# Tile 0 of a convolution and two-layer block on one core: four rows a partition loaded, four moved across partitions by TensorE

## The chip, the cores and the metric

The kernel runs on one core of one Trainium2 chip. The metric is device time in microseconds, a median of runs; it was 696.64 us before (three runs, 696.33 to 697.31). The engines are TensorE (PE; its weight loads are PEld), VectorE (DVE), ScalarE (ACT), GpSimd (POOL) and SyncE (SP), which issues nearly all transfers.

## What is computed

```python
# batch 2, 4160 positions, 192 channels, 8 heads, 7 taps, 1024 hidden
w = softmax(weight_gen, axis=-1)                      # [2, 4160, 8, 7]
out = np.einsum('bshk,bskhg->bshg', w, x_unf)         # x_unf: the 7 latest rows of x
xk = mu_k * x + (1 - mu_k) * x_prev                   # x = out; x_prev: one position earlier
k = np.maximum(xk @ w_k, 0.0)
x = sigmoid(xr @ w_r) * (k * k @ w_v)
h = np.maximum(x @ w_in, 0.0)
return h * sigmoid(conv3(h)) @ w_out                  # conv over 3 positions
```

Every position first takes a weighted sum of seven rows of x ("tokens" below), is then mixed with the position before, and goes through two feed-forward layers.

## The kernel before

The 4160 positions are cut into ten tiles (238, 238, seven of 476, 352), each for both batches. Tile 0 has SLOTS = 2 tokens a partition: partition p holds tokens 2p and 2p + 1, and, as each token needs six rows ahead of it, L + PAD = 2 + 6 = 8 rows of 192 f32. They come in one load a batch (line 575), of 128 x 8 x 192 x 4 bytes; neighbouring partitions load six rows in common. `rows_r` has two buffers, so that tile 1's first load reuses tile 0's first buffer.

`attention` (line 569) makes each token. A product of 128 x 1344 (7 x 192) multiplies seven rows with the softmax weights `sw` (line 583), for tile 0, batch 0 on VectorE and for everything else on GpSimd, into one of two `prod` buffers. For tile 0 (and three tokens of tile 1) the seven parts are added by TensorE: seven products with the identity matrix in plain f32 (line 590, two records each in the trace), copied by ScalarE to `tok` (lines 596, 597). `mixing` (line 616) transposes the tokens, mixes them with the previous position and splits each value into two parts, high and low, that TensorE takes in its faster f32 form. `moe1_half` and `moe1` are the first layer, `moe2` the second.

The weights are loaded in pieces during the first 50 us or so (`fetch`, line 404) and split in high and low parts on ScalarE, VectorE and TensorE (`narrow`, line 433, and `split`, line 454). The piece `w_k` comes first. `softmax` (line 536) runs on VectorE for tiles 0 to 2: a TENSOR_REDUCE, a subtraction, an exponential on ScalarE, a second TENSOR_REDUCE, and so on.

PSUM has eight banks. `pa_r` (line 379) hands out pa0, pa1 and pc1 in turn until plan time 26; the sums and the transposes of tile 0 take theirs from it, in the order of the list below.

The order of work comes from a planner. Each step is put down with a plan time (`at`, line 387); these times give a first order in which buffers are handed out. `Program.schedule` (line 136) then takes all operations, finds their dependencies by overlap of regions, and plans forwards and backwards for ROUNDS rounds with costs of its own (`cost`, line 97): a GpSimd product of 1344 elements costs 0.135 + 1344 / 446 us (line 132), a VectorE one 0.065 + 1344 / 960 (line 123). These are multiplied by PACE of the engine (line 149). SLACK (line 185) is added where TensorE waits for another engine's result, and 3.507 us stand for the end of a transfer (lines 223, 234). Each engine's queue is then issued in the planned order and runs in that order on the chip.

Ahead of TensorE's first operation `warm` (line 1078) puts WARM = 26 products of 128 x 256 whose result nobody reads. `identity` (line 1001) makes the 128 x 128 identity matrix on GpSimd.

Of the kernel before, what the change touches and what calls it, by code (L numbers as in the profile page):

```python
# [12 lines left out]
ALU = mybir.AluOpType  # L13
AX = mybir.AxisListType

NB, SEQ, DM, NH, KS, DFF = 2, 4160, 192, 8, 7, 1024
# [8 lines left out]
PART = [128] * NTILE  # L25
SLOTS = [2, 2] + [4] * 7 + [3]
EXTRA = [0] + [p * l - n for p, l, n in zip(PART, SLOTS, SIZES)][1:]
PAD = KS - 1
WIN = KS * DM
NF = DFF // 128  # L30
LAG = 12
WARM = 26
SLACK = {"ACT": 0.311, "DVE": 0.274, "POOL": 0.239}
PACE = {"ACT": 1.045, "DVE": 1.035, "POOL": 1.037}
ROUNDS = 13
HELD = [85.0, 140.0, 215.0, 290.0, 365.0, 440.0, 515.0]
HIGH = range(5)
LOWS = {(NTILE - 1, NB - 1, k) for k in range(6, NF)}
# [15 lines left out]
class Program:  # L54
# [4 lines left out]
        self.ops, self.spaces = [], {}  # L59
        self.real = {"PE": nc.tensor, "ACT": nc.scalar, "DVE": nc.vector, "POOL": nc.gpsimd, "SP": nc.sync}  # L60

    warm = None

    def engine(self, name):
        program = self
# [70 lines left out]
    def schedule(self):  # L136
        n = len(self.ops)
        succ, left, ready, dur, late, moved = [[] for _ in range(n)], [0] * n, [0.0] * n, [0.0] * n, [0.0] * n, [0.0] * n
        shares = [False] * n
        log = {}  # L140
        for i, (eng, method, a, k, _, hold) in enumerate(self.ops):
            ready[i] = hold
            aps = [x for x in [*a, *k.values()] if hasattr(x, "tensor") and hasattr(x, "ap")]
            out = k["out"] if "out" in k else aps[0]
# [14 lines left out]
            for x, write in [(x, False) for x in ins] + [(out, True)]:  # L159
# [3 lines left out]
                for e in seen:  # L163
                    j, w, q0, q1, g0, g1 = e
# [16 lines left out]
        load = [op[1] == "dma_start" for op in self.ops]  # L181
        turns = [op[2][2] if op[0] == "ACT" and op[1] == "activation" and op[2][2] in (ACTF.Exp, ACTF.Sigmoid) else None
                 for op in self.ops]
        hold = ready
# [23 lines left out]
        def forward(rank):  # L208
            nonlocal when
            when = hold[:]  # L210
            start, last, table = [0.0] * n, 0.0, ACTF.Exp
            wires = dict.fromkeys(self.real, 0.0)

            def step(i, eng, t):
                nonlocal last, table
                start[i] = t
                if turns[i] is not None:
                    t = t + (0.0 if turns[i] == table else 1.3)
                    table = turns[i]
                end = t + late[i]  # L220
                if load[i]:
                    wires[eng] = max(wires[eng], t + dur[i] + 0.55) + moved[i]
                    end = wires[eng] + 3.507
                last = max(last, end)
                for j in succ[i]:
                    when[j] = max(when[j], t + dur[i] if eng in ("PE", "POOL") and eng == name[j] else end + slack(i, name[j]))
                return t

            walk((pred, succ), lambda i: (rank[i], i), step)
            return start, last  # L230

        def backward(start, last):
            nonlocal when
            full = [dur[i] + 0.55 + moved[i] + 3.507 if load[i] else late[i] for i in range(n)]
            when = [full[i] - dur[i] for i in range(n)]
            rank = [0.0] * n

            def step(i, eng, t):
                rank[i] = last - t - dur[i]
                for j in pred[i]:  # L240
                    when[j] = max(when[j], t + dur[i] - dur[j] + (dur[j] if name[j] in ("PE", "POOL") and name[j] == eng else full[j] + slack(j, eng)))
                return t

            walk((succ, pred), lambda i: (-start[i], -i), step)
            return rank

        when = []
        start, last = forward([op[4] for op in self.ops])
        for _ in range(ROUNDS):
            start, last = forward(backward(start, last))  # L250
        for i in sorted(range(n), key=lambda i: (start[i], i)):
            eng, method, a, k = self.ops[i][:4]
            if eng == "PE" and self.warm:
                self.warm = self.warm()
            getattr(self.real[eng], method)(*a, **k)  # L255


# [12 lines left out]
def conv_moe_kernel(ctx: ExitStack, tc: tile.TileContext, xp, wg_first, wg_rest, w_k, w_v, w_r, w_in, conv_w, w_out, out):  # L270
# [6 lines left out]
    def new(name, shape, dtype=F32):  # L277
        t = sb.tile(shape, dtype, name=name)
        prog.spaces[t.tensor.name] = "SBUF"
        return t  # L280
# [24 lines left out]

    onemu = new("onemu", [128, 4])
    cw = new("cw", [128, 3, NF])
    ident = new("ident", [128, 128])

    signs = new("signs", [128, 256], F32R)  # L310
    wkA = new("wkA", [128, 2, DFF], F32R)
# [19 lines left out]
    prod_r = ring("prod", 2, [128, WIN])  # L331
# [55 lines left out]
    def at(t, fn, hold=0.0):  # L387
        plan.append((t, len(plan), fn, hold))
# [180 lines left out]
    def attention(i, b, t_load, t, dt_, eng, hold=(0.0, 0.0)):  # L569
        L = SLOTS[i]  # L570

        def load():
            rows_t[i, b] = rows_r()[:, :L + PAD]
            row = b * (SEQ + PAD) + STARTS[i] - EXTRA[i]
            SP.dma_start(out=rows_t[i, b], in_=bass.AP(tensor=xp.tensor, offset=xp.offset + row * DM, ap=[[L * DM, PART[i]], [1, (L + PAD) * DM]]))

        def token(l):
            if i not in tok_t:
                tok_t[i] = tok_r()
            p = prod_r()  # L580
            y = p.rearrange("p (k d) -> p k d", k=KS)
            w = sw[:, sum(slots[:i]) + b * L + l].unsqueeze(2).to_broadcast([128, KS, DM // NH, NH])
            eng.tensor_tensor(p.rearrange("p (k g h) -> p k g h", k=KS, h=NH),
                              rows_t[i, b][:, l:l + KS].rearrange("p k (g h) -> p k g h", h=NH), w, op=ALU.mult)
            if i < 1 or (i, b, l) in SUMS:

                def total():
                    z = pa_r()[:, :DM]
                    for k in range(KS):
                        PE.matmul(z, lhsT=ident, rhs=y[:, k], start=(k == 0), stop=(k == KS - 1))  # L590
                    x = tok_t[i][:, :, b * DM:b * DM + DM]
                    if i:
                        ACT.copy(x[:, l], z)
                        return
                    m, r = 64 * b, 128 - 128 * b
                    ACT.copy(x[:, l, m:m + 128], z[:, m:m + 128])
                    ACT.copy(x[:, L + l, 0:128].rearrange("p (k d) -> p k d", k=2), z[:, r:r + 64].unsqueeze(1).to_broadcast([128, 2, 64]))


                now = t + l * dt_  # L600
                later((now + 0.2) // 1 + 0.8 if i else now, total)
                return
            eng.tensor_tensor(y[:, 0:3], y[:, 0:3], y[:, 3:6], op=ALU.add)
            eng.tensor_tensor(y[:, 0:2], y[:, 0:2], y[:, 2:7:4], op=ALU.add)
            eng.tensor_tensor(tok_t[i][:, l, b * DM:b * DM + DM], y[:, 0], y[:, 1], op=ALU.add)

        at(t_load, load, hold[0])
        for l in range(L):
            at(t + l * dt_, lambda l=l: token(l), hold[1])

# [388 lines left out]
        DVE.tensor_scalar(onemu, mu, -1.0, 1.0, op0=ALU.mult, op1=ALU.add)  # L999

    def identity():
        POOL.memset(ident, 0.0)
        POOL.affine_select(out=ident, in_=ident, compare_op=ALU.not_equal, fill=1.0, base=0,
                           pattern=[[-1, 128]], channel_multiplier=1)
        ACT.copy(signs[:, 0:128], ident)
        ACT.activation(signs[:, 128:256], ident, ACTF.Copy, scale=-1.0)

# [66 lines left out]
    while plan:  # L1074
        t, _, fn, hold = heapq.heappop(plan)
        prog.now, prog.hold = t, hold
        fn()
    def warm():
        for _ in range(WARM):
            nc.tensor.matmul(ar_r.tiles[0][:, 0:256], lhsT=signs[:, 0:128], rhs=signs[:, 0:256], start=True, stop=True)  # L1080

    prog.warm = warm
# [65 lines left out]
```

## Time and profile before

| what | value |
|---|---|
| median of three runs | 696.64 us |
| the profiled execution | 696.22 us |
| its span in the trace | 694.4 us |
| TensorE busy | 683.8 us (98%) |
| VectorE busy | 590.0 us (85%) |
| ScalarE busy | 630.3 us (91%) |
| GpSimd busy | 531.3 us (77%) |

The span runs from the first to the last instruction; the execution's own time has 1.8 us more around it. An engine's busy time is the time in which at least one of its instructions ran. A product of TensorE holds some latency after its last column has entered, so a TensorE that reads as busy can still wait between products that hang on one another.

### The profile page before, as it was taken

Reading aid. Unit: us, or ns where it says so; the run is one execution under the profiler, and the core shown is the slowest. Engines: PE = TensorE matmul, PEld = TensorE weight load, DVE = VectorE, ACT = ScalarE, POOL = GpSimd, SP = SyncE. Lnnn points to the kernel's source line nnn. Section 1 sums busy time; section 2 is a strip of 40 time slices with the busy share of each in tenths; the row PEclk is TensorE's granted clock in tenths of the full one; section 3 lists DMA queues with packets and bytes.
Section 4 is the critical chain, followed back from the end, with each engine's and each line's share of the span. In section 5 each row is a group of like instructions: output and inputs, shape, how many; then the busy total and the mean of one; then the engine's idle time right before and its main releaser. Section 6 shows DMA issues by size and latency. Waiting matters only on the chain.

```text
span 694.4 us, 10540 instructions
## 1 busy us (share of the span) xinstructions
PE 683.8 (98%) x3473; PEld 603.0 (87%) x3473; DVE 590.0 (85%) x1003; ACT 630.3 (91%) x1333; POOL 531.3 (77%) x388
## 2 busy tenths in 40 slices
PE   8999999999999999999999999999999999999997
PEld 7799887888888888888888888888888888899997
DVE  7999998889879888988798978988897768686787
ACT  4988999999999998999999899898999999999996
POOL 3899999996998799669976997599929996243335
PEclk9999999999999999999999999999999999999999
DMA  8886021222021310130212112121202000200010
GB/s 298 262 210 236 23 68 42 72 86 63 8 86 64 86 65 29 65 86 13 79 65 71 24 57 93 35 54 57 80 22 71 8 28 14 65 8 28 6 33 31
DMA packets 20790, 48.43 MB, mean 70 GB/s; under 512 B 3456, under 2 KB 16256, under 8 KB 20608
## 3 DMA queue, kind: packets, MB, share of 16 engines
q1 hardware_dynamic: 20592, 47.58, 23.2%
q8 instruction: 27, 0.44, 0.3%
q14 instruction: 27, 0.22, 0.1%
q10 hardware_dynamic: 144, 0.18, 0.1%
HBM read 27.40 MB, written 6.39 MB: 49 GB/s over the span
## 4 chain that ended last, share of the span: by engine, by line
PE 86%; DVE 7%; ACT 4%; issue 1%; DMA 1%; SPq 0%; DVEq 0%; ACTq 0%
PE pa L255 25%; PE pc L255 21%; PE bm L255 13%; PE am L255 12%; PE br L255 8%; PE ar L255 7%; DVE pc L255 2%; DMA sw<-in_rest_dram 1%; DVE stage L255 1%; DVE g L255 1%; DVE s L255 1%; ACT pc L255 1%; ACT pa L255 1%; DVE mk L255 0%; DVE ar L255 0%
## 5 line engine op out<-in xcount | busy, mean ns | idle before, releaser
L255 POOL TENSOR_TENSOR prod<-rows,sw 128x1344 f32<-128x1344 f32 x68 | 210.3, 3092 | 13.7 <-PE pa L255 11.1
L255 DVE SCALAR_TENSOR_TENSOR pc<-h,cw,pc 128x476 f32<-128x476 f32 (+1 forms) x276 | 193.7, 704 | 27.2 <-ACT pc L255 24.4
L255 ACT ACTIVATE pa<-pa 128x476 f32<-128x476 f32 (+2 forms) x280 | 151.8, 546 | 11.5 <-PE pa L255 9.0
L255 POOL TENSOR_TENSOR prod<-prod 128x576 f32<-128x576 f32 (+1 forms) x126 | 154.2, 1224 | 8.4
L255 PE MATMUL bm<-g,wo 128*128 128x476 f32 (+1 forms) x411 | 135.2, 376 | 0.4 <-ACT stage L255 0.4
L255 PE MATMUL am<-s,wv 128*128 128x476 f32 (+2 forms) x464 | 129.8, 357 | 0.0
L255 PE MATMUL pa<-xA,wkA 128*128 128x476 f32 (+2 forms) x438 | 112.0, 360 | 0.8 <-DVE s L255 0.8
L255 PE MATMUL pc<-x,wiA 128*128 128x478 f32 (+1 forms) x414 | 111.8, 375 | 0.4 <-ACT x L255 0.2
L255 DVE TENSOR_TENSOR s<-pa,s 128x476 fp32r<-128x476 f32 (+1 forms) x137 | 86.7, 634 | 19.5 <-ACT s L255 18.6
L255 PE MATMUL br<-g,wo 128*128 128x476 f32 (+1 forms) x274 | 100.6, 375 | 0.0
L255 PE MATMUL ar<-s,wv 128*128 128x476 f32 (+2 forms) x336 | 99.8, 350 | 0.0
L255 ACT ACTIVATE h<-pc 128x478 f32<-128x478 f32 (+1 forms) x138 | 78.4, 569 | 17.8 <-PE pc L255 16.6
L255 ACT ACTIVATE pc<-h,cw 128x476 f32<-128x476 f32 (+1 forms) x138 | 91.7, 665 | 0.8
L255 ACT ACTIVATE pc<-pc 128x476 f32<-128x476 f32 (+1 forms) x152 | 84.3, 555 | 8.3 <-DVE pc L255 4.5
L255 POOL TENSOR_TENSOR g<-stage,g 128x476 fp32r<-128x476 f32 (+1 forms) x41 | 47.5, 1160 | 56.0 <-ACT g L255 44.1
L255 PEld LDWEIGHTS pa<-xA,wkA 128*128 128x128 f32 x438 | 79.0, 188 | 12.2 <-DVE s L255 1.3
L255 PEld LDWEIGHTS am<-s,wv 128*128 128x128 f32 x464 | 81.0, 188 | 9.3
L255 PEld LDWEIGHTS pc<-x,wiA 128*128 128x128 f32 x414 | 76.3, 188 | 11.7 <-DVE g L255 1.0
L255 PEld LDWEIGHTS bm<-g,wo 128*128 128x128 f32 x411 | 76.5, 188 | 11.2 <-ACT stage L255 0.8
L255 PE MATMUL pa<-xB,wkB 128*128 128x476 f32 (+2 forms) x292 | 82.7, 359 | 0.0
L255 PE MATMUL pc<-x,wiB 128*128 128x478 f32 (+1 forms) x276 | 81.7, 376 | 0.0
L255 ACT CAST s<-pa 128x476 fp32r<-128x476 f32 (+1 forms) x137 | 76.4, 558 | 1.1
(170 smaller groups left out, 1177.5 us busy)
## 6 DMA issues: line engine op xcount, KB each, us to landing
rows<-in_x_dram SPq DMA_DIRECT2D x14, 960.0 KB, 4.9
xB<-rm SPq DMA_DIRECT2D x28, 119.0 KB, 2.2
rows<-in_x_dram SPq DMA_DIRECT2D x4, 768.0 KB, 6.3
xB<-mk SPq DMA_DIRECT2D x16, 119.0 KB, 2.3
rows<-in_x_dram SPq DMA_DIRECT2D x2, 864.0 KB, 5.5
r<-r SPq DMA_DIRECT2D x14, 119.0 KB, 2.2
x<-x SPq DMA_DIRECT2D x14, 119.0 KB, 2.2
out_dram<-stage SPq DMA_DIRECT2D x7, 238.0 KB, 2.0
```

The costliest lines, as they stand in the source:

```text
L255: getattr(self.real[eng], method)(*a, **k)
```

## The change

Tile 0 loads only the first four of the eight rows of a partition (n = 2 L = 4), half the bytes. Rows 4 to 7 of partition p are rows 0 to 3 of partition p + 2; `shift` makes them on TensorE, by a product in plain f32 with an identity matrix that is moved by two columns (`next2`, out of a matrix of 128 x 130), in two halves of 384 columns, each copied from PSUM to the rows buffer by ScalarE. That is four products and four copies for the two batches. The products of batch 0 are made in two parts for each token: first those of the loaded rows (four taps of token 0, three of token 1), then those of the shifted ones (three and four). The warm-up products become eight ahead of TensorE's first operation, none ahead of its second and 14 ahead of its third. The planner's constants change: SLACK, PACE, ROUNDS and the constant at the end of a transfer.

```diff
+SHIFTED = (0,)
-WARM = 26
-SLACK = {"ACT": 0.311, "DVE": 0.274, "POOL": 0.239}
-PACE = {"ACT": 1.045, "DVE": 1.035, "POOL": 1.037}
-ROUNDS = 13
+WARM = 8, 0, 14
+SLACK = {"ACT": 0.324, "DVE": 0.3, "POOL": 0.515}
+PACE = {"ACT": 1.055, "DVE": 1.01, "POOL": 0.995}
+ROUNDS = 8
...
-                    end = wires[eng] + 3.507
+                    end = wires[eng] + 3.71
...
-            full = [dur[i] + 0.55 + moved[i] + 3.507 if load[i] else late[i] for i in range(n)]
+            full = [dur[i] + 0.55 + moved[i] + 3.71 if load[i] else late[i] for i in range(n)]
...
-            if eng == "PE" and self.warm:
-                self.warm = self.warm()
+            if eng == "PE" and self.fills:
+                self.warm(self.fills.pop(0))
...
-    ident = new("ident", [128, 128])
+    wide = new("ident", [128, 130])
+    ident, next2 = wide[:, 0:128], wide[:, 2:130]
...
-            SP.dma_start(out=rows_t[i, b], in_=bass.AP(tensor=xp.tensor, offset=xp.offset + row * DM, ap=[[L * DM, PART[i]], [1, (L + PAD) * DM]]))
-
-        def token(l):
+            n = 2 * L if i in SHIFTED else L + PAD
+            SP.dma_start(out=rows_t[i, b][:, :n], in_=bass.AP(tensor=xp.tensor, offset=xp.offset + row * DM, ap=[[L * DM, PART[i]], [1, n * DM]]))
+
+        def shift():
+            r = rows_t[i, b].rearrange("p k d -> p (k d)")
+            for j in (0, 2 * DM):
+                z = pa_r()[:, :2 * DM]
+                PE.matmul(z, lhsT=next2, rhs=r[:, j:j + 2 * DM], start=True, stop=True)
+                ACT.copy(r[:, j + 4 * DM:j + 6 * DM], z)
+
+        prod = {}
+
+        def token(l, part=None):
             if i not in tok_t:
                 tok_t[i] = tok_r()
-            p = prod_r()
+            if part != 1:
+                prod[l] = prod_r()
+            p = prod[l]
+            k0, k1 = (0, KS) if part is None else ((0, 4 - l), (4 - l, KS))[part]
             y = p.rearrange("p (k d) -> p k d", k=KS)
-            w = sw[:, sum(slots[:i]) + b * L + l].unsqueeze(2).to_broadcast([128, KS, DM // NH, NH])
-            eng.tensor_tensor(p.rearrange("p (k g h) -> p k g h", k=KS, h=NH),
-                              rows_t[i, b][:, l:l + KS].rearrange("p k (g h) -> p k g h", h=NH), w, op=ALU.mult)
+            w = sw[:, sum(slots[:i]) + b * L + l, k0:k1].unsqueeze(2).to_broadcast([128, k1 - k0, DM // NH, NH])
+            eng.tensor_tensor(y[:, k0:k1].rearrange("p k (g h) -> p k g h", h=NH),
+                              rows_t[i, b][:, l + k0:l + k1].rearrange("p k (g h) -> p k g h", h=NH), w, op=ALU.mult)
+            if part == 0:
+                return
             if i < 1 or (i, b, l) in SUMS:
...
         at(t_load, load, hold[0])
+        if i in SHIFTED:
+            at(-96 + 6 * b if i == 0 else t - 0.5, shift)
+        if (i, b) == (0, 0):
+            for part in range(2):
+                for l in range(L):
+                    at(t + (2 * part + l) * 0.03, lambda l=l, part=part: token(l, part), hold[1])
+            return
...
-        POOL.memset(ident, 0.0)
-        POOL.affine_select(out=ident, in_=ident, compare_op=ALU.not_equal, fill=1.0, base=0,
-                           pattern=[[-1, 128]], channel_multiplier=1)
+        POOL.memset(wide, 0.0)
+        POOL.affine_select(out=wide, in_=wide, compare_op=ALU.not_equal, fill=1.0, base=0,
+                           pattern=[[-1, 130]], channel_multiplier=1)
...
-    def warm():
-        for _ in range(WARM):
+    def warm(n):
+        for _ in range(n):
```

## Rows read from the trace of the kernel before

**Rows 1.** The page: busy time of each engine, and the chain by engine.

```profile
PE 683.8 (98%) x3473; PEld 603.0 (87%) x3473; DVE 590.0 (85%) x1003; ACT 630.3 (91%) x1333; POOL 531.3 (77%) x388
...
PE 86%; DVE 7%; ACT 4%; issue 1%; DMA 1%; SPq 0%; DVEq 0%; ACTq 0%
```

**Rows 2.** Busy time by stretch: stretch and length, engines, granted clock, transfers' share, GB/s.

```profile
2.50:6.00 3.50, 3.41 (x16) 3.41 (x17) 2.58 (x8) 0.43 (x2) 0.00 (x0) 1.00 1.01 359
6.00:10.00 4.00, 3.81 (x27) 3.64 (x27) 3.96 (x4) 0.64 (x1) 0.00 (x0) 1.00 0.97 354
...
7.64:22.35 14.71, 14.68 (x79) 12.49 (x80) 14.03 (x27) 9.98 (x31) 10.37 (x4) 1.00 1.02 296
22.00:26.00 4.00, 2.92 (x13) 1.67 (x12) 3.85 (x9) 3.18 (x10) 4.00 (x3) 1.00 0.96 324
22.00:120.00 98.00, 93.90 (x608) 83.25 (x607) 91.40 (x178) 88.44 (x205) 91.34 (x65) 1.00 0.45 136
```

**Rows 3.** The chain in order of time, first 25 us: start, us, what.

```profile
3.21 7.57 DMA sw<-in_rest_dram
...
17.44 0.62 ACT xA L255 x2
...
24.95 1.10 PE bm L255 x2
```

**Rows 4.** VectorE's timeline: start, us, instruction, idle time before it and its releaser.

```profile
5.52 0.39 DVE L255 TENSOR_TENSOR sw<-sw,am 128x224 f32<-128x224 f32 x1
5.94 3.03 DVE L255 TENSOR_TENSOR prod<-rows,sw 128x1344 f32<-128x1344 f32 x2
...
10.80 0.57 DVE L255 TENSOR_REDUCE am<-sw 128x32 f32<-128x224 f32 x1 [0.51 <-DMA sw<-in_rest_dram]
```

**Rows 5.** SyncE's timeline: when the first transfers are issued.

```profile
1.19 0.42 SPq L255 DMA_DIRECT2D rows<-in_x_dram  x1
1.65 0.43 SPq L255 DMA_DIRECT2D stage<-in_moe_w_k_dram  x1
2.13 0.43 SPq L255 DMA_DIRECT2D rows<-in_x_dram  x1
```

**Rows 6.** Transfers issued from 1 to 3.3 us: KB, us from issue to landing.

```profile
rows<-in_x_dram SPq DMA_DIRECT2D x1, 768.0 KB, 4.2
stage<-in_moe_w_k_dram SPq DMA_DIRECT2D x1, 512.0 KB, 5.7
...
rows<-in_x_dram SPq DMA_DIRECT2D x1, 768.0 KB, 7.0
...
sw<-in_rest_dram SPq DMA_DIRECT2D x1, 112.0 KB, 7.6
```

**Rows 7.** ScalarE's timeline, 7 to 15 us.

```profile
7.33 0.64 ACT L255 ACTIVATE bm<-stage 128x512 f32<-128x512 f32 x1 [3.08 <-DMA stage<-in_moe_w_k_dram]
10.46 0.65 ACT L255 ACTIVATE br<-stage 128x512 f32<-128x512 f32 x1 [2.50 <-DMA stage<-in_moe_w_k_dram]
11.04 0.43 ACT L255 COPY tok<-pa 128x128 f32<-128x128 f32 x2
...
14.81 0.53 ACT L255 ACTIVATE bm<-stage 128x384 f32<-128x384 f32 x1
```

**Rows 8.** TensorE's timeline: warm-up products early and late, first sums, one f32 product.

```profile
2.59 3.35 PE L1080 MATMUL ar<-signs 128*128 128x256 f32 x14 [2.59 <-ACT signs L255]
...
6.23 1.23 PE L1080 MATMUL ar<-signs 128*128 128x256 f32 x9
...
7.64 3.16 PE L255 MATMUL pa<-prod,ident 128*128 128x192 f32 x18 [0.19 <-DVE prod L255]
...
17.92 0.81 PE L255 MATMUL bm<-stage,ident 128*128 128x384 f32 x2
```

**Rows 9.** GpSimd's timeline: its first products, with the idle time before them.

```profile
10.25 3.04 POOL L255 TENSOR_TENSOR prod<-rows,sw 128x1344 f32<-128x1344 f32 x1 [8.89 <-PE pa L255]
13.90 3.05 POOL L255 TENSOR_TENSOR prod<-rows,sw 128x1344 f32<-128x1344 f32 x1 [0.61 <-PE pa L255]
17.99 3.05 POOL L255 TENSOR_TENSOR prod<-rows,sw 128x1344 f32<-128x1344 f32 x1 [1.04 <-DVE g L255]
```

More of the change, by code (lines that the diff above doesn't have):

```diff
@@ L60, in __init__ @@
         self.real = {"PE": nc.tensor, "ACT": nc.scalar, "DVE": nc.vector, "POOL": nc.gpsimd, "SP": nc.sync}
-    warm = None
+    warm, fills = None, list(WARM)
     def engine(self, name):
```

## The prediction

> **What bounds the kernel now.** I read the page first, then the stretches, then the chain, then each queue's timeline over the first 30 us. The page says that TensorE is busy 98% of the span and carries 86% of the chain [rows 1]; an edit that touches tile 0 alone can therefore pay only by letting TensorE's dense work begin earlier, or by filling its gaps. The stretches show where gaps are: from 22 to 120 us TensorE stands idle 98.00 - 93.90 = 4.10 us, 1.08 of them between 22 and 26, and VectorE and GpSimd are then busy 91.40 and 91.34 of 98 us [rows 2]. So the start is a place where three engines and the transfers (97 to 101% busy from 2.5 to 10 us [rows 2]) are all near full. The chain starts with a transfer: it stands on the load of the second weights piece from 3.21 us for 7.57 us [rows 3], that is until VectorE's TENSOR_REDUCE at 10.80. VectorE had stood still for 0.51 us before that instruction, and the row names this load as what ended the wait [rows 4]. From there VectorE and then ScalarE carry the chain to 24.95 us, where TensorE takes it over [rows 3]; TensorE is busy 14.68 of 14.71 us from 7.64 to 22.35 [rows 2].
>
> **The transfers.** Two loads of 768 KB become 384 KB. From 2.5 to 6 us the transfers move 359 GB/s [rows 2], so 393,216 bytes less are 1.10 us, 2.19 us for both. By issue and time to landing, the rows of batch 0 landed at 1.19 + 4.2 = 5.4 us and should land near 4.3; those of batch 1 landed at 2.13 + 7.0 = 9.1 and should land near 6.9; the softmax weights' second piece landed at 3.21 + 7.6 = 10.8 and should land near 8.6 [rows 3, 5, 6]. What is gained by each depends on who waits. Batch 0's first product began at 5.94, when the softmax weights (5.52 + 0.39) were ready, half a microsecond after its rows [rows 4]: nothing there. The w_k piece landed at 1.65 + 5.7 = 7.35 and ScalarE took it at 7.33 [rows 5 to 7]; it would come a microsecond earlier, but VectorE, which needs ScalarE's result next, is in the products until 9.0: nothing. The reduce at 10.80 is the one wait for a transfer on the path: **-0.51 us**. SyncE issues as many transfers as before; its next load, of tile 1, reuses the first rows buffer and waits for the last product piece, 0.14 us later (below), with the later weight loads queued behind it; the queue is 2.19 us emptier, which covers that.
>
> **The products in pieces.** Two instructions of 1344 elements become four of 768, 576, 576 and 768. One of 1344 ran 3.03 us for two; one of 224 ran 0.39 [rows 4]. Line through both: (1.55 - 0.39) / 1120 = 1.04 ns an element, so 0.96, 0.76, 0.76, 0.96 = 3.44 us, less three overlaps of 0.08 (two of 1.55 took 3.03): about 3.2, **+0.14 us** on VectorE. That is on the path. Below by the elements alone: 0. Above, a full drain for each new instruction: 0.3.
>
> **The shift on TensorE and ScalarE.** Four matrix products of 384 columns in plain f32, of which one ran 0.81 us, both its records together, at the high clock [rows 8]. Before, TensorE filled the time from 2.59 us to the first sum at 7.64 with 26 warm-up products; the first 14 took 3.35 us, nine later ones 1.23 us [rows 8], so 256 columns go in about 0.21 us first and 0.12 afterwards, the levels of 1.2 and 2.4 GHz, with the change near 5.95 us. The page's granted clock reads 1.00 in every stretch [rows 2] and does not show this. Eight warm-up products end near 2.59 + 8 x 0.21 + 0.2 = 4.5, just when the rows should be there. Two shifts at 0.64 apart at the high level and double that at the low one run until about 6.5 if the level rises as before, and the second copy ends near 7.2 (a ScalarE copy of 384 columns out of PSUM takes 0.53 [rows 7]). The third piece of the products, the first that needs those rows, begins at 5.94 + 0.88 + 0.68 = 7.5: the margin is 0.3 us. ScalarE was idle 3.08 us ahead of 7.33 and 2.50 ahead of 10.46 [rows 7]; the four copies (2.1 us) fit there, and if they don't, the w_k conversions behind them slip by up to 0.5.
> Fourteen more warm-up products take 14 x 0.12 = 1.65 us and hold TensorE to about 8.1, where the sums began at 7.64 [rows 8]. Batch 1's shift (two products, 1.29 us of array time) falls into the full stretch to 22.35. So TensorE gets **1.8 us more** there; 1.08 us of idle time stand at 22 to 26 [rows 2], and sums that start later find both tokens' first pieces made. Ends: 0 if order and gaps take all of it, +1.8 if none. I take 0 on the path, because VectorE and ScalarE, not TensorE, carry the chain from 10.8 to 24.95 [rows 3].
> The identity matrix of 130 instead of 128 columns costs GpSimd some nanoseconds long before it is used: nothing; its cover is GpSimd's idle time until 10.25 [rows 9].
>
> **The new plan.** The constants change the order of the whole program, and no row shows that order. Bounds: the 4.10 us of idle time of TensorE from 22 to 120 [rows 2] could shrink by half (-2.0), or grow by as much as TensorE's extra (+1.8). The sign I read from paces: a product is planned at 0.135 + 1344/446 = 3.15 us times 1.037 = 3.26 on GpSimd and ran 3.04 to 3.05 [rows 9]; times 0.995 it is 3.13. VectorE's is planned at 1.465 x 1.035 = 1.52 and ran 3.03 / 2 [rows 4]; times 1.01 it is 1.48. Both come nearer. I take an eighth of the idle time, **-0.55 us**, nearer to nothing than to either end.
>
> **Sum.** -0.51 + 0.14 - 0.55 = -0.92 us. The profiled execution took 696.22 us (694.4 of span and 1.8 around it), so 695.30 in its terms; the median of the runs shown is 0.42 above it, so **695.7 us**.
>
> **Rivals.**
> *The lead is used in full.* If the order turns the whole 2.19 us of transfers into earlier weights and no engine takes it back, the start moves by 2.2 to 2.7 us: 696.6 - 2.4 = **694.2**. For it: transfers 97 to 101% busy. Against: VectorE, which is busy 91.40 of the 98 us from 22 on [rows 2] and carries the chain before [rows 3].
> *GpSimd starts late.* Three banks (pa0, pa1, pc1) serve shifts and sums in turn: the fourth shift product gets the bank of token 0's sums, so it waits for them and for their copy. Sums from 8.1 for 2.4 us, a copy of 0.43 [rows 7], 0.81 and 0.53 for the shift: GpSimd's first product, which needs batch 1's shifted rows, starts near 12.4 instead of 10.25 [rows 9]. Its own waits of 0.61 and 1.04 us [rows 9] absorb 1.65 of the 2.2; with TensorE's extra of 1.8 in the same sums, tile 1's tokens come 0.5 to 2.3 us later. It decides from the point where the delay at 17.99 us exceeds VectorE's gain of 0.37. Then 696.6 + 1.8 = **698.4**, slower.
> *The clock.* From 2.59 us TensorE ran without a stop until it reached the high level near 5.95 [rows 8]; now a transfer is waited for between fillers and shift. Were the level low when the sums start, token 0's 14 records (18 took 3.16 us, so about 2.4 for 14 [rows 8]) would take 4.8: 2.4 us more, 0.4 of it made good by VectorE's gain: **698.6**.
> The Trainium skill's page "TensorE: Matmul & The Clock Gate" says in "Why this matters for your kernels" that idle stretches between bursts of products put the array back to half rate, which speaks against cutting the fillers; the rows agree as far as they go, since the uninterrupted fillers did end at the high level, and no run here shows a gap at that place.
> *Hidden anyway.* If the 0.51 us only moves the wait to the next instruction, the time is that of before, 696.6 less a few tenths: **696.4**.
>
> **How the numbers follow.** A measurement of this kernel can tell 0.2%, 1.4 us, from no change: faster is under 695.25, slower over 698.03. The forecast has 0.46, spread about 1 us either way, so a third of it (0.16) is faster and the rest (0.30) within. Full lead 0.25, all faster. Hidden 0.11, within. GpSimd late 0.12 and clock 0.06, slower. Sums: faster 0.41, same 0.41, slower 0.18. The range leaves out the slower rivals' centres and the best of the full lead: 693.6 to 697.6; the forecast's own is 694.7 to 696.8.
>
> **What would show it.** Right: the rows of batch 0 land by 4.5 us, the reduce on the second weights piece has no wait for a transfer, the third product piece begins by 7.6, TensorE's sums by 8.3, and TensorE's idle time of 22 to 120 us shrinks by some half microsecond. Wrong: ScalarE's copies end after 7.5 and VectorE waits for them; sums go at twice the spacing; GpSimd's first product starts after 12 us and its later ones keep the delay. The forecast falls on the fast side if the dense stretch begins 2 us earlier, or if the new order closes gaps late in the program, which no row of the start could tell.

## The result, and the profile after

The changed kernel took **701.82 us** (median of four runs, 701.20 to 702.62) against 696.50 for the kernel before (four runs). The ratio is 1.0074, 95% interval 1.0059 to 1.0089: 5.3 us slower. The forecast was 695.7 us with a range of 693.6 to 697.6; it has the wrong sign and the range misses the time. Five more runs later gave 702.04 us, ratio 1.0076 (1.0062 to 1.0090). The profiled execution took 701.97 us (span 700.2), 5.75 more than the one before.

The page of the kernel after, busy times and the chain by engine:

```profile
PE 687.1 (98%) x3477; PEld 605.9 (87%) x3477; DVE 589.6 (84%) x1005; ACT 631.3 (90%) x1337; POOL 530.8 (76%) x388
...
PE 91%; ACT 3%; DVE 3%; POOL 1%; DMA 1%; issue 1%; DVEq 0%
```

Against [rows 1], TensorE's share of the chain rises from 86 to 91%, and VectorE's falls from 7 to 3%: up to 17.8 us the early stretch that VectorE and ScalarE carried is now TensorE's.

TensorE's timeline of the kernel after (start, us, instruction, then idle time before it and its releaser):

```profile
2.59 2.07 PE L1104 MATMUL ar<-signs 128*128 128x256 f32 x8 [2.59 <-ACT signs L256]
4.59 2.90 PE L256 MATMUL pa<-rows,ident 128*128 128x384 f32 x4
6.72 2.59 PE L1104 MATMUL ar<-signs 128*128 128x256 f32 x14
9.14 0.81 PE L256 MATMUL pa<-rows,ident 128*128 128x384 f32 x2
9.79 2.44 PE L256 MATMUL pc<-prod,ident 128*128 128x192 f32 x14
...
13.57 0.81 PE L256 MATMUL pc<-rows,ident 128*128 128x384 f32 x2
...
25.52 0.58 PE L256 MATMUL pa<-xA,wkA 128*128 128x238 f32 x3
```

Read it against [rows 8]. There the sums began at 7.64; here at 9.79, 2.15 us later, with shift products, 14 warm-up products and batch 1's first shift in front of them. An f32 product is two records: batch 0's two shift products, four records, take 2.90 us, where one product took 0.81 at the high level [rows 8], so they ran at 1.2 GHz. The 14 warm-up products behind them are called fillers below. Their spacing falls from 0.21 to 0.12 us only near 7.7 us; before it did so near 5.95. The first product of the first layer (pa<-xA,wkA) starts at 25.52, where the kernel before had its like at 22.35.

The same kernel's VectorE:

```profile
6.05 0.96 DVE L256 TENSOR_TENSOR prod<-rows,sw 128x768 f32<-128x768 f32 x1
8.04 1.43 DVE L256 TENSOR_TENSOR prod<-rows,sw 128x576 f32<-128x576 f32 x2 [1.03 <-ACT rows L256]
...
9.98 0.95 DVE L256 TENSOR_TENSOR prod<-rows,sw 128x768 f32<-128x768 f32 x1
...
12.64 0.55 DVE L256 TENSOR_REDUCE am<-sw 128x32 f32<-128x224 f32 x1
```

The wait for a transfer ahead of the reduce, 0.51 us in [rows 4], is gone. In its place VectorE waits 1.03 us for ScalarE's second copy of shifted rows. VectorE's queue holds token 0's second piece ahead of token 1's first, so a piece that needs no shifted row stands behind one that does.

ScalarE's copies, and GpSimd's first products:

```profile
6.25 0.48 ACT L256 COPY rows<-pa 128x384 f32<-128x384 f32 x1 [1.88 <-PE pa L256]
7.53 0.48 ACT L256 COPY rows<-pa 128x384 f32<-128x384 f32 x1 [0.80 <-PE pa L256]
...
14.42 0.48 ACT L256 COPY rows<-pc 128x384 f32<-128x384 f32 x1 [1.72 <-PE pc L256]
```

```profile
14.98 6.07 POOL L256 TENSOR_TENSOR prod<-rows,sw 128x1344 f32<-128x1344 f32 x2 [13.62 <-ACT rows L256]
```

GpSimd starts at 14.98 against 10.25 [rows 9]. Its rows come from the fourth shift product (bank pc, 13.57), behind token 0's sums in that bank and their copy.

Busy times by stretch (columns as in rows 2), kernel before and kernel after:

```profile
22.00:70.00 48.00, 45.50 (x349) 42.50 (x348) 46.18 (x104) 41.35 (x107) 43.76 (x31) 1.00 0.77 232
70.00:120.00 50.00, 48.40 (x261) 40.74 (x260) 45.22 (x75) 47.09 (x98) 47.57 (x35) 1.00 0.15 44
```

```profile
22.00:70.00 48.00, 44.59 (x340) 42.03 (x339) 45.73 (x102) 42.09 (x114) 44.39 (x31) 1.00 0.86 243
70.00:120.00 50.00, 47.24 (x266) 41.55 (x265) 44.60 (x76) 43.96 (x91) 48.59 (x34) 0.97 0.15 40
```

TensorE's idle time in these 98 us grows from 2.50 + 1.60 = 4.10 to 3.41 + 2.76 = 6.17 us. So there are two candidates: about 3.2 us are lost by the first layer's first product, and some 2 us in gaps that mostly lie behind tile 0. The second group shows in TensorE's waits (us in total, times, longest):

```profile
PE ar L256 <- ACT s L256: 2.2, 2, 1.9
PE pa L256 <- DMA wkB<-x: 1.2, 1, 1.2
PE pc L256 <- DVE ar L256: 0.9, 1, 0.9
PE pc L256 <- ACT x L256: 0.9, 1, 0.9
```

### The profile page after: what moved, and what is told of

Read it like the earlier page. It is cut to its first block, busy times and chain, and to the rows that moved or that the text cites. A ratio compares the mean times of both kernels' runs of the same rounds, so it can differ in the third digit from the quotient of the medians.

```text
span 700.2 us, 10537 instructions
## 1 busy us (share of the span) xinstructions
PE 687.1 (98%) x3477; PEld 605.9 (87%) x3477; DVE 589.6 (84%) x1005; ACT 631.3 (90%) x1337; POOL 530.8 (76%) x388
## 4 chain that ended last, share of the span: by engine, by line
PE 91%; ACT 3%; DVE 3%; POOL 1%; DMA 1%; issue 1%; DVEq 0%
PE pa L256 27%; PE pc L256 22%; PE bm L256 13%; PE am L256 12%; PE br L256 9%; PE ar L256 8%; POOL prod L256 1%; DMA stage<-in_moe_w_out_dram 1%; ACT pa L256 1%; PE ar L1104 1%; ACT s L256 0%; DVE ar L256 0%; DVE stage L256 0%; ACT att L256 0%; ACT pc L256 0%
## 5 line engine op out<-in xcount | busy, mean ns | idle before, releaser
L256 ACT ACTIVATE pa<-pa 128x476 f32<-128x476 f32 (+2 forms) x286 | 155.0, 547 | 16.3 <-PE pa L256 14.4
L256 PE MATMUL pa<-xA,wkA 128*128 128x476 f32 (+2 forms) x456 | 116.7, 359 | 0.8 <-DVE mk L256 0.8
L256 DVE TENSOR_TENSOR s<-pa,s 128x476 fp32r<-128x476 f32 (+1 forms) x140 | 88.3, 632 | 9.7 <-ACT s L256 8.2
L256 PEld LDWEIGHTS pa<-xA,wkA 128*128 128x128 f32 x456 | 81.9, 190 | 11.9 <-ACT pc L256 0.9
L256 ACT ACTIVATE pc<-pc 128x476 f32<-128x476 f32 (+1 forms) x146 | 80.8, 554 | 7.8 <-DVE pc L256 7.4
L256 PE MATMUL pa<-xB,wkB 128*128 128x476 f32 (+2 forms) x304 | 86.0, 357 | 1.2 <-DMA wkB<-x 1.2
L256 ACT CAST s<-pa 128x476 fp32r<-128x476 f32 (+1 forms) x140 | 78.1, 559 | 0.8
```

## The experiments

Theories: **delay** (TensorE's later start costs what it is late), **order** (the new constants make a worse order of everything), and **GpSimd late** (the rival of the prediction). In what follows "full clock" means runs with a mean granted clock of 0.999 or 1.000.

### Parts of the change, in the planner's own orders

**consts_only**: the kernel before with the new constants alone.

```diff
-SLACK = {"ACT": 0.311, "DVE": 0.274, "POOL": 0.239}
-PACE = {"ACT": 1.045, "DVE": 1.035, "POOL": 1.037}
-ROUNDS = 13
+SLACK = {"ACT": 0.324, "DVE": 0.3, "POOL": 0.515}
+PACE = {"ACT": 1.055, "DVE": 1.01, "POOL": 0.995}
+ROUNDS = 8
...
-                    end = wires[eng] + 3.507
+                    end = wires[eng] + 3.71
```

> The kernel before with nothing of the change but the planner's new constants (SLACK, PACE, ROUNDS, 3.71). If the new order of the rest is what costs the 5.3 us (theory: plan), this takes 700 to 702 us with the first sums still at 7.6 us and GpSimd's first product still near 10.3. If the late shift of batch 1 is what costs (theory: GpSimd late), this stays within 1.5 us of the kernel before, 695 to 698.

Measured 701.05 us (699.81 to 702.48, four runs), ratio 1.0063 (1.0044 to 1.0082). The two runs at full clock took 700.74 and 699.81, so 3 to 4 us come from the order alone. Its sums begin at 7.61 and its first layer at 22.64, close to the 7.64 and 22.35 of the kernel before: the loss lies behind the start.

**shift_old_consts**: the changed kernel with the old constants (that diff reversed).

> The changed kernel with the planner's old constants. Plan: back to 696 to 698 us although GpSimd's first product still starts after 13 us. GpSimd late: that product starts near 15 us as in the changed kernel and the time stays at 700 us or more.

Measured 709.19 us (708.32 to 711.05), ratio 1.0184 (1.0168 to 1.0201). With the old constants the new work gets an order with long waits: TensorE waits 3.3 us for ScalarE's `tok`, 3.0 for its `s`. For the changed list the new constants are much the better ones, by 7 us, though for the old list they cost 4.5. What constants are worth depends on the list, and the parts of this change do not add up.

**fill_none**: the changed kernel without the 14 fillers. The order of all other instructions is the same.

```diff
-WARM = 8, 0, 14
+WARM = 8, 0, 0
```

> The changed kernel without the 14 warm-up products ahead of TensorE's third operation; the order of everything else is the same. Theory fillers: batch 1's first shift product starts near 7.2 us instead of 9.15 and the sums 2 us earlier, the time falls by 1.5 to 2 us to about 700. GpSimd late: GpSimd's product moves with the sums, from 15.0 to about 13, and the time falls by no more than 2 us. Clock: if the sums run at the low level without the fillers (records 0.32 us apart instead of 0.16), nothing is gained: 701 to 703. Plan: 701.8 unchanged.

Measured 701.14 us (698.36 to 701.86, four runs), ratio 1.0058. The run at full clock took 698.36; the others, at 0.995 to 0.998, took 700.86 to 701.86. In its profile, which is the run at full clock, the first layer starts 1.83 us before the changed kernel's 25.52 (row below), and GpSimd at 12.71 in place of 14.98.

```profile
23.69 0.58 PE L256 MATMUL pa<-xA,wkA 128*128 128x238 f32 x3
```

**shift_early**: both shifts ahead of the tokens in the list, so that batch 1's gets its banks before the sums.

```diff
-            at(-96 + 6 * b if i == 0 else t - 0.5, shift)
+            at(-96 + 0.1 * b if i == 0 else t - 0.5, shift)
```

> The changed kernel with both batches' shifts ahead of the tokens in the plan's first order, so that the fourth shift product takes the bank of the first instead of that of token 0's sums. GpSimd late: its first product starts near 11.5 us instead of 15.0 and the time falls by 2 to 3.5 us, to 698.5 to 700. Plan: a start of GpSimd 3 us earlier changes little, 701 to 702.

Measured 704.99 us (704.50 to 710.38), ratio 1.0138. GpSimd moves only from 14.98 to 14.43, because batch 1's shift now stands at 10.56, ahead of all sums, which begin at 11.85, and GpSimd's row names TensorE's sums (`pa`) as what ended its wait. It is another order besides, and the profiled execution was the longest of the four (710.38 us, clock 0.988). This run says nothing clean of "GpSimd late"; the next ones hold the order.

### The same order, one thing changed

For the next runs the planner works on the old list with the old constants, and only when the instructions are issued are those of tile 0 replaced. All others stand in each queue exactly where they stood in the kernel before. Batch 0's shift uses banks bm and br, batch 1's ar and pc1, so that no shift waits for a sum, and VectorE makes both pieces that need no shifted row first.

```diff
-            eng, method, a, k = self.ops[i][:4]
+            for eng, method, a, k in self.swaps.get(i) or [self.ops[i][:4]]:
...
+        first = shift(0, (bm_r.tiles[0], br_r.tiles[0]))
+        out[prod_at[0, 0][0]] = first + [piece(0, 0), piece(1, 0), piece(0, 1)]
+        out[prod_at[0, 1][0]] = [piece(1, 1)]
+        i = sum_at[0, 0]
+        out[i] = shift(1, (ar_r.tiles[0], pc_r.tiles[1])) + [prog.ops[i][:4]]
```

**old_order_shift**: all of the change except constants, in the old order.

> The change's work (half loads, both shifts, products in pieces, warm-up 8 and 14) in exactly the order that the kernel before issues everything else in; the shifts stand ahead of the first sums, in banks of their own, and both first pieces ahead of the second ones. Theory order (what the planner does with the rest costs 4 us or more, the shift itself little): 696 to 698.5 us, the first sums 1 to 2.5 us later than before. Theory shift (the shift's own work on TensorE and ScalarE and the late GpSimd cost it): 700 us or more although the order is the old one.

Measured 700.59 us (699.78 to 700.95, four runs), ratio 1.0057 (1.0042 to 1.0072). Here the order is the old one, and still 3.8 us are lost; none of its runs was at full clock (0.996 and 0.997). Its TensorE:

```profile
6.78 2.53 PE L1088 MATMUL ar<-signs 128*128 128x256 f32 x14
9.15 0.81 PE L255 MATMUL ar<-rows,ident 128*128 128x384 f32 x2
9.80 0.81 PE L255 MATMUL pc<-rows,ident 128*128 128x384 f32 x2
10.44 3.09 PE L255 MATMUL pa<-prod,ident 128*128 128x192 f32 x18
```

The sums begin 2.80 us later than at 7.64 [rows 8], and the first layer 2.45 us later (24.80).

**old_order_lead**: only the half loads, which end earlier (the lead). The rows that are not loaded are set to 0 by GpSimd in place of the shift, so the kernel leaves out tile 0's taps on them.

```diff
+            out[load_at[b]].append(("POOL", "memset", (rows_t[0, b][:, 2 * L:], 0.0), {}))
```

> The old order with the half loads alone: no shift, no pieces, 26 warm-up products; the four rows that aren't loaded are set to zero by GpSimd, which is idle then, so tile 0's result leaves out the taps of those rows. It prices the lead of 2.2 us of transfers. If the lead is worth what the prediction took, -0.5 us or a little more: 695.5 to 696.3 us, and the reduce on the second weights piece no longer waits. If the whole lead counts: 694 to 695. If it is hidden: 696.3 to 697.

Measured 696.46 us (695.88 to 700.22, ten runs), ratio 1.0008 (0.9991 to 1.0026): no change that can be told. Its VectorE does what the prediction said of the transfers; the reduce comes 0.52 us earlier than in [rows 4] and waits for nothing:

```profile
9.68 0.69 DVE L255 TENSOR_SCALAR pc<-stage 128x512 uint32<-128x512 uint32 x1
10.28 0.56 DVE L255 TENSOR_REDUCE am<-sw 128x32 f32<-128x224 f32 x1
```

The six runs at full clock took 695.88 to 696.48 us, some 0.3 to 0.9 under the 696.77 of the kernel before, measured beside it. So a gain near the predicted 0.51 can be there, though in the profile (a full-clock run) the first layer starts only 0.26 us earlier, at 22.09; the four runs at a lower clock, 698.17 to 700.22, take more than that away.

**old_order_pieces**: only the products in pieces, with full loads and 26 warm-up products.

> The old order with the products of batch 0 in pieces alone (all eight rows loaded, 26 warm-up products, no shift). By the prediction +0.14 us on VectorE; token 0's product is complete 0.8 us later, which holds its last sums. Theory delay: 696.7 to 697.5 us. If pieces cost nothing: 696.5.

Measured 697.91 us (697.20 to 701.65, ten runs), ratio 1.0018 (1.0007 to 1.0029). The eight runs at full clock lie at 697.20 to 698.10, about 1.0 us over the 696.67 of the kernel before, where 0.14 was predicted. The profiled execution was a long one, 701.65 us, and shows why it was long, not why the others were 1 us over: TensorE stood 3.37 us for the transfer of `wkB` (first row, its timeline), and ran at the lower level behind that (second, busy times from 28 to 32 us, granted clock 0.50).

```profile
27.61 0.54 PE L255 MATMUL pc<-xB,wkB 128*128 128x238 f32 x1 [3.37 <-DMA wkB<-x]
```

```profile
28.00:32.00 4.00, 4.00 (x14) 2.97 (x14) 2.70 (x7) 0.95 (x3) 2.67 (x1) 0.50 0.96 332
```

**old_order_batch0**: half load, shift and pieces for batch 0 alone, with eight warm-up products.

> The old order with the half load, the shift and the pieces for batch 0 alone; batch 1 loads its eight rows; warm-up 8 and none later. Sums near 8 us instead of 7.64, GpSimd's first product near 10.6. Theory delay: 0.5 to 1.2 us more than before, 697 to 697.9 us. Rival (the shift as such costs, wherever it lies): 698.5 or more.

Measured 697.43 us (697.14 to 701.53, seven runs), ratio 1.0031 (1.0011 to 1.0051); at full clock (four runs) 697.14 to 697.43, about 0.6 us over. In its profile, a run of 700.96 us at a lower clock, the sums begin at 7.24, earlier than before, and the loss comes as in old_order_pieces, with a wait of 2.87 us for `wkB`. Where TensorE is not made late, half load, shift and pieces of a batch cost some tenths.

**old_order_no_fill**: old_order_shift without the 14 fillers.

```diff
-WARM = 8, 0, 14
+WARM = 8, 0, 0
```

> old_order_shift without the 14 warm-up products between the two batches' shifts. Theory delay: batch 1's shift starts near 7.2 us, the first sums near 8.5 to 9 instead of 10.44, so 1.5 to 2 us less than old_order_shift: 698 to 699 us. Clock rival: without them the high level comes later and the sums run at half pace: 700 us or more.

Measured 699.98 us (698.11 to 700.31, five runs), ratio 1.0039 (1.0026 to 1.0052). The fillers are not what makes this one late: TensorE then waits 1.33 us for batch 1's rows at 8.80, since its shift stands ahead of the first sum, and the sums begin at 10.20 in place of 10.44. That is the profile of a run at 0.997; the two runs at full clock took 698.11 and 698.23, 1.5 us over the 696.67 of the kernel before. When the sums began in those two is not recorded.

**delay_only**: the kernel before with 50 warm-up products in place of 26, and nothing else.

```diff
-WARM = 26
+WARM = 50
```

> The kernel before with 50 warm-up products instead of 26 and nothing else: the same order, and the first sums held back by 24 x 0.12 = 2.8 us, to about 10.4 us, where old_order_shift has them. Theory delay (a later start of TensorE's sums is passed on in full to the end): 2.5 to 2.8 us more, 699.2 to 699.6 us, and up to 701 if the clock falls on the way as in old_order_shift. Rival (later gaps absorb it): under 1 us more, below 697.8.

Measured 701.40 us (700.32 to 703.43, four runs at clocks of 0.995 to 0.997), ratio 1.0072 (1.0054 to 1.0089). No transfer, product or order is changed here; TensorE only begins late, and it costs what old_order_shift costs:

```profile
2.59 8.31 PE L1080 MATMUL ar<-signs 128*128 128x256 f32 x50 [2.59 <-ACT signs L255]
10.74 3.09 PE L255 MATMUL pa<-prod,ident 128*128 128x192 f32 x18
...
25.08 0.58 PE L255 MATMUL pc<-xA,wkA 128*128 128x238 f32 x3
```

3.10 us late at the sums are 2.73 at the first layer. GpSimd's first product is 3.02 us late as well (13.27), behind these sums; but the chain, followed back from the end of the run, does not pass GpSimd there. It goes from TensorE by ScalarE to a transfer into `wkB`, one of the first layer's weights, and on to TensorE:

```profile
2.59 8.31 PE ar L1080 x50
10.90 2.93 PE pa L255 x18
...
18.52 8.96 DMA wkB<-x
```

The profiled execution, the fastest of the four, is 4.1 us over the profiled one of the kernel before, and the rest of that comes close behind the first layer: busy times from 28 to 32 us, first of the kernel before, then of delay_only, then of old_order_shift.

```profile
28.00:32.00 4.00, 3.91 (x22) 3.28 (x22) 3.66 (x8) 4.00 (x12) 2.38 (x2) 1.00 0.75 268
```

```profile
28.00:32.00 4.00, 4.00 (x17) 2.93 (x16) 3.68 (x9) 2.02 (x7) 3.84 (x4) 0.60 1.03 399
```

```profile
28.00:32.00 4.00, 4.00 (x17) 3.20 (x16) 3.41 (x9) 1.93 (x7) 2.75 (x3) 0.57 1.05 392
```

The granted clock is 0.60 and 0.57, so most of these 4 us ran at 1.2 GHz, and the transfers are at 1.03 and 1.05 where the kernel before had 0.75. From about 37 us to the end both traces stand a constant 4.1 and 4.0 us behind the kernel before. No run here has the delay of delay_only at full clock, so its price without that stretch is not shown.

### The order alone

**new_order_no_shift**: the order of the changed kernel, held as above, but with the shift products and their copies taken out, full loads, and 26 warm-up products ahead. The pieces stay.

```diff
-WARM = 8, 0, 14
+WARM = 26, 0, 0
...
+                prog.swaps[len(prog.ops)] = prog.swaps[len(prog.ops) + 1] = []
                 PE.matmul(z, lhsT=next2, rhs=r[:, j:j + 2 * DM], start=True, stop=True)
                 ACT.copy(r[:, j + 4 * DM:j + 6 * DM], z)
```

> The order of the changed kernel with its shift products, copies and half loads taken out (all eight rows loaded, 26 warm-up products, pieces kept). Theory order: 699 to 702 us, nearly as slow as the changed kernel. Theory shift: back to 696 to 698 us.

Measured 703.35 us (699.77 to 706.58, five runs), ratio 1.0095 (1.0065 to 1.0126). The profiled run, at full clock, took 699.77, the others (clock 0.993 to 0.998) 702.01 to 706.58. Without a shift 3 us are still lost. Of these some 0.7 are the late clock of this execution: its 26 warm-up products took 5.92 us where the kernel before took 4.87 (last section), and its sums began at 8.31. TensorE has the same waits as in the changed kernel (for ScalarE's `s` 2.2 us, for its `x` 0.9, for VectorE's `ar` 0.9). They belong to the order:

```profile
22.00:70.00 48.00, 44.17 (x338) 41.28 (x337) 45.26 (x101) 42.16 (x112) 43.68 (x31) 1.00 0.81 240
70.00:120.00 50.00, 47.22 (x269) 41.20 (x268) 45.50 (x76) 45.28 (x94) 48.51 (x35) 1.00 0.15 44
```

**old_slack_up**: the kernel before with one constant moved by 3%.

```diff
-SLACK = {"ACT": 0.311, "DVE": 0.274, "POOL": 0.239}
+SLACK = {"ACT": 0.321, "DVE": 0.274, "POOL": 0.239}
```

> The kernel before with one constant moved a little (SLACK of ScalarE 0.311 to 0.321 us), which gives another order of the same work. If the plan found for the old constants is a good draw among very uneven ones (theory order): 698 to 704 us. If orders of neighbouring constants are worth the same: 696 to 697.5 us.

Measured 701.61 us (701.47 to 702.66, four runs), ratio 1.0076 (1.0061 to 1.0091), three of the runs at full clock. TensorE is idle for 4.50 and 4.42 us in the two stretches, where the kernel before had 2.50 and 1.60:

```profile
22.00:70.00 48.00, 43.50 (x325) 40.24 (x325) 43.32 (x96) 40.73 (x106) 42.60 (x31) 1.00 0.81 234
70.00:120.00 50.00, 45.58 (x262) 39.57 (x261) 45.12 (x78) 44.25 (x92) 48.43 (x35) 1.00 0.14 39
```

**planner_rounds**: the kernel before with `ROUNDS = 12` in place of 13.

> The kernel before with 12 planning rounds in place of 13 and nothing else, another order made with the old constants. If the order of the kernel before is one good draw among uneven ones: 699 to 703 us. If the old constants give good orders as a rule and only the changed ones are bad: 696 to 697.5 us.

Measured 701.83 us (699.93 to 702.59, four runs), ratio 1.0069 (1.0055 to 1.0084). A third other order of the same work, again 3 to 6 us over.

### How the 5.3 us divide

Open is the division, since delay and order each cost nearly the whole alone. Two kernels have the same order, with and without the 14 fillers.

**fill_none_again** and **after_again**: the kernels fill_none and after unchanged, five runs each.

> The kernel after without its 14 later warm-up products, in more executions. If the delay of TensorE's sums is what costs, and the order of the rest only the remainder, executions at a granted clock of 1.0 come at 698 to 699 us, about 3 us below those of the changed kernel at the same clock, and the remaining 1.5 to 2.5 us over the kernel before belong to the order and the pieces. If the one execution of 698.36 us was chance and the order carries nearly all of the 5.3 us, executions at full clock come at 700.5 to 701.5 us.

> The changed kernel once more, beside the one without its 14 warm-up products. If the delay costs about 3 us: 701 to 702 us at a granted clock of 1.0, 3 us over the other kernel at the same clock. If the order carries nearly all: no more than 0.8 us apart at the same clock.

Measured 700.08 us (698.70 to 700.22) and 702.04 us (700.46 to 702.73). With the four earlier runs of each, at full clock: without fillers 698.36, 698.70, 698.82 and 700.08 (median 698.76), with them 700.46, 701.20, 701.66 and 702.04 (median 701.43). The fillers cost 2.7 us by these medians; by all nine runs of each, 700.16 against 701.97, it is 1.8, and that is also what the two pairs of profiles show directly at the first layer's first product: 1.83, and here 25.86 - 24.13 = 1.73.

```profile
24.13 0.58 PE L256 MATMUL pa<-xA,wkA 128*128 128x238 f32 x3
```

```profile
25.86 0.58 PE L256 MATMUL pa<-xA,wkA 128*128 128x238 f32 x3
```

(First fill_none_again, then after_again.) The other part, 698.76 less 696.7 (the kernel before had medians of 696.54 and 696.78 beside them), some 2.1 us at full clock, is order, shift and pieces together. The 0.5 us that remain of the 5.3 are executions below full clock and spread.

The traces point at the order for much of the 2.1. From the first sum to the first layer TensorE takes 22.35 - 7.64 = 14.71 us in the kernel before and 24.80 - 10.44 = 14.36 in old_order_shift, with the whole shift; in the new order it takes 23.69 - 7.52 = 16.17 in fill_none and 24.22 - 8.31 = 15.91 in new_order_no_shift, without a shift. So some 1.2 us come with the new order and its pieces there, and 0.3 with the shift; each figure is one execution.

## Why the prediction was wrong

**What bounds the kernel: read rightly, and then not used.** The page said that TensorE is busy 98% of the span and that an edit to tile 0 pays only if TensorE's dense work begins earlier. By that rule the 1.8 us more for TensorE ahead of the first layer had to be the first term of the sum.

**The transfers, -0.51: the mechanism held.** The rows landed 3.3 and 3.8 us after their issue, the second softmax piece 6.5 after its own at 3.07, that is at 9.6 (8.6 forecast), ahead of the reduce. (Batch 1's rows landed at 5.4 and not 6.9, as the new plan issues them ahead of the w_k piece; in the old order, in old_order_shift and old_order_no_fill, they landed at 7.8 and 8.7.) The wait went, in the changed kernel and in old_order_lead. But in the changed kernel the reduce itself came later, at 12.64 instead of 10.80, so nothing was gained there. At the end the lead alone leaves 0.3 to 0.9 us in full-clock runs, and nothing that can be told over all its runs.

**The pieces, +0.14: right on VectorE, too small at the end.** Run behind one another, in old_order_pieces, the four took 3.17 us against 3.03, the forecast to the hundredth; in the changed kernel, with a wait and another instruction between them, 0.96 + 1.43 + 0.95 = 3.34. But in the old order they cost about 1.0 us at the end, and the path from 0.14 to that is not shown.

**The shift taken as 0 on the path: the step that failed.** "I take 0 on the path, because VectorE and ScalarE, not TensorE, carry the chain from 10.8 to 24.95" took the chain of the old kernel as if it stayed. TensorE was busy 14.68 of 14.71 us in that stretch [rows 2], so any delay of it comes out at the far end: delay_only turns 3.10 us into 2.73 at the first layer. The term itself was too small too: its +1.8 was 0.5 us in front of the sums and 1.3 for batch 1's shift behind them, and the first layer came 3.17 us late, with sums at 9.79 instead of 8.1. The fillers alone took 2.59 us, not 1.65, and half of batch 1's shift stood ahead of the sums. (That the fillers cost 1.8 by the profiles is a coincidence with that +1.8.) With the low level at 28 us, in the old order, a delay cost more than its own length. The details failed with it: batch 0's second copy ended at 8.0 and not 7.2, as the high level came at 7.7 in this execution instead of 5.95, and VectorE's queue asked for the shifted rows in its second piece, not its third. So the margin of 0.3 became a wait of 1.03; in old_order_shift, with the forecast's order of pieces, it was 0.49. The copies took 0.48 us, not 0.53; the row read for that is one from `stage` into `bm`, not out of PSUM.

**The new plan, -0.55: wrong in sign.** This is the second step that failed. The reading under it was half wrong: GpSimd's pace came nearer to its rows, but VectorE's planned 1.52 us already was the measured 3.03 / 2, and 1.48 is further off (an eighth of 4.10 is also 0.51 and not 0.55). And paces are no sign of a better order: consts_only has the new ones and costs 4.5 us. The bounds (-2.0 to +1.8) were too narrow too, as they came from idle time inside 22 to 120 us; a 3% step of one constant moves the whole by 5.

**The rivals.** "GpSimd starts late" named the place exactly (fourth shift product in the bank of token 0's sums) and GpSimd came later than it said, 14.98 against 12.4. What that wait costs by itself is not shown: fill_none has it as well (GpSimd at 12.71) and takes 698.8 at full clock, but with the new order in it, and in delay_only, where GpSimd is as late as TensorE's sums, the chain passes it by. "The clock" was right that the level would be lower for longer, wrong in place: it was the shift products, not the sums, that ran at it. "The lead in full" and "hidden" fell. The chance of 0.18 for slower was far too small for a kernel whose order is made anew.

**What stays open**: why pieces alone cost 1 us, how the 2.1 us divide exactly between order and tile 0's own work, and which of a queue's transfers holds `wkB` back.

## What to carry to other kernels

Where a planner orders a whole program, a new constant or a new step is a new draw of the order; hold the order and swap only the changed instructions before anything is said of an edit. On an engine that is busy without a gap, work put in front of it is paid nearly in full at the end of the busy stretch (2.73 of 3.10 us in delay_only), whoever carries the chain in the old profile. Filler products are a cheap probe of that: 24 more of them delay the engine without touching the program, though here a stretch at the lower clock came with them.

## What was not expected of the hardware

**The granted clock falls inside a dense program in some executions.** The kernel before had clocks of 0.999 or 1.000 in nearly all its runs. Nearly every variant had executions below that, mostly at 0.995 to 0.998, most of them 1.5 to 4 us longer than full-clock ones of the same kernel (old_order_pieces: 697.20 to 698.10 against 700.23 and 701.65). The stretches at 1.2 GHz follow waits of TensorE: 3.37 us for `wkB` in old_order_pieces; 0.58 us for the same copies, after one of 0.54, in delay_only; and in the changed kernel the one shown here, in TensorE's timeline, with the busy times of 80 to 90 us (granted clock 0.83) below it.

```profile
81.87 0.60 PE L256 MATMUL ar<-s,wv 128*128 128x238 f32 x3 [1.86 <-ACT s L256]
```

```profile
80.00:90.00 10.00, 8.14 (x45) 7.44 (x45) 7.95 (x14) 7.80 (x16) 9.84 (x8) 0.83 0.17 38
```

after_again, the same program, had the same wait and kept the high level:

```profile
81.75 0.60 PE L256 MATMUL ar<-s,wv 128*128 128x238 f32 x3 [1.88 <-ACT s L256]
```

```profile
80.00:90.00 10.00, 8.25 (x54) 7.58 (x55) 8.99 (x16) 8.73 (x19) 9.84 (x8) 1.00 0.17 38
```

So the length of such a gap alone does not decide it. The Trainium skill's page "TensorE: Matmul & The Clock Gate" ("Why this matters for your kernels") says that idle gaps between bursts put the array back to half rate. The trace agrees as to the kind of place, but waits of 0.58 and 1.86 us are shorter than the gaps that page warns of, and the pair above shows that the program does not settle it.

**The rise of the clock comes at another time in every execution.** The same 26 uninterrupted warm-up products took 4.69 us in consts_only, 4.87 in the kernel before, 5.43 in planner_rounds and 5.92 in new_order_no_shift, where they stand 0.21 us apart to the end, as at the low level. The rows are of the kernel before and of new_order_no_shift:

```profile
2.59 4.87 PE L1080 MATMUL ar<-signs 128*128 128x256 f32 x26 [2.59 <-ACT signs L255]
```

```profile
2.59 5.92 PE L1107 MATMUL ar<-signs 128*128 128x256 f32 x26 [2.59 <-ACT signs L256]
```

So the rise near 7.7 us in the changed kernel lies within this spread, and no run shows that the shift products and their waits put it off. First sums of one program differ by it too: 7.52 us in fill_none and 8.30 in fill_none_again.

**A copy inside the core can land late.** The copies into `wkB` (inside SBUF, 256 KB each) landed 6.5 us after their issue in the kernel before (median of four) and 8.5 us in old_order_pieces, with the queue's packets at 97.6 and 103.5% of the transfer engines' time from 10 to 30 us. TensorE's wait of 3.37 us for one of them was the longest inside that run.
